# Half-row projections and query features, paired into two PSUM banks and issued as one burst per step

## The chip, the cores and the metric

The kernel runs on one core of a Trainium2 chip. The time is the device time of one execution in microseconds (us). The kernel before was timed beside every experiment of a call (one round of building and timing some kernels together), on the same chip; the calls ran on several chips, so a difference of two medians from different calls is rough. Its runs of one call spread by 2 to 5%, so verdicts rest on ratios: the mean time of one kernel's fast runs over the mean of the other's fast runs of the same rounds, with a 95% interval. That is not quite the ratio of the medians, which are quoted too. A run counts as slow when it lies over 1.5% above the fastest run of the same kernel; slow runs are in the medians, not in the ratios.

## The reference, cut to what matters

```python
def phi(x):                                    # x: q or k, (8 batches, 8 heads, 576 rows, 64)
    proj = np.einsum('bhsd,df->bhsf', x, w_phi)            # 64 -> 128
    proj = proj - np.max(np.abs(proj), axis=-1, keepdims=True)
    return np.concatenate([np.exp(proj), np.exp(-proj)], axis=-1)

q_p, k_p = phi(q), phi(k)
kv  = np.einsum('bhsf,bhsd->bhfd', k_p, v);  z = np.sum(k_p, axis=2)
num = np.einsum('bhsf,bhfd->bhsd', q_p, kv); den = np.einsum('bhsf,bhf->bhs', q_p, z)[..., None] + 1e-06
x = num / den                                  # then a second layer per batch, 512 wide:
h = np.maximum(x @ w_in, 0.0)                  # u and v are its halves
v_n = (v - mean) / np.sqrt(var + 1e-06)        # mean and var of v's rows
out = (u * (w_spatial @ v_n + b_spatial)) @ w_out
```

The contraction of each projection has 64 terms; TensorE has 128 rows.

## The kernel before

Work is cut into 36 units of eight 128-row blocks of q and k: 32 "pair" units (two heads of one batch, four blocks each) and 4 units of leftover rows (64 rows of each head, of two batches). Batches 0 to 7 have four units each; bN.j below is unit j of batch N, TN a unit of leftover rows. A step of the program handles one new unit, later parts of older units, and "fills" in matmuls of the second layer of finished batches. The turned q and k (kT, qT) hold two blocks one above the other, 64 rows each, and the weights are a block-diagonal matrix wphi2, so half of what TensorE multiplies is zero:

```python
def by_token(xT, half):                        # keys and queries alike
    ps = psum.tile([P, 4, F], FP32, tag="bank", name="ps")
    for x in range(2):
        nc.tensor.matmul(out=ps[:, 2 * x:2 * x + 2, :], lhsT=xT[:, 2 * half + x, :], rhs=wphi2, start=True, stop=True)
    return ps
...
def a_qfeat(u):                                # query features, and sel @ mT subtracts the row maxima
    for half in range(2):
        pq = psum.tile([P, 4, P], FP32, tag="bank", name="pq")
        for par in range(2):
            nc.tensor.matmul(out=pq[:, 2 * par:2 * par + 2, :], lhsT=wphi2[:, par * F:(par + 1) * F],
                             rhs=u["qT"][:, 2 * half:2 * half + 2, :], start=True, stop=False)
            ...                                # two matmuls with sel
        ...                                    # qf = exp(pq), exp(-pq) on ScalarE
...
ORDER = (("keys", 0.375), ("queries", 0.25), ("attention", 0), ("sums", 0.25),
         ("next", 0.125), ("features", 0), ("out", 0), ("maxima", 0))   # the number: share of the fill after it
```

After the keys come their row maxima on VectorE (mk), their exponentials on ScalarE (kf), and em = exp(-mk), exp(mk), with which GpSimd scales v (vs).

The inputs arrive in the background, by a table that counts in units ahead of their use. k and q are loaded by GpSimd's queue (which casts them to 2 bytes), v by SyncE's, and `cross` turns k and q of batches 2 to 7 by a DMA transpose on SyncE's queue into kT_b and qT_b:

```python
AT, AB, XP = 4, 5, 2
at(u["i"] - AT, load_tail, "k", u["g"]);   at(u["i"] - AT + 1, load_tail, "q", u["g"])   # leftover rows
at(u["i"] - AB, load, "k", u["b"]);        at(u["i"] - AB + 1, load, "q", u["b"])        # a batch
at(u["i"] - AB + 1, load_v, u["b"], nc.sync)
at(u["i"] - XP, cross, u["b"])
```

All PSUM tiles take turns in eight banks.

## Time and profile before

| | before |
|---|---|
| median of the first three runs | 289.92 us (286.92 to 296.59) |
| span in the profile | 286.4 us |
| PE / ScalarE / VectorE / GpSimd busy | 91% / 80% / 70% / 64% |
| last em (unit 35) starts at | 225.38 us |

PE's waits for loads (line, in total, times, longest), asked for from 60 us on to leave out the start, show one alone:

```profile
PE ps L232 <- DMA qT_b<-q_bf: 1.4, 1, 1.4
```

### The profile page before, as it was taken

The numbers are of one execution on the slowest core, as the hardware profiler recorded it, in microseconds if no ns is written. First come the engines' busy times: TensorE is split into PE (matmuls) and PEld (weight loads), VectorE is DVE, ScalarE is ACT, GpSimd is POOL, SyncE is SP. The second block draws the span as 40 slices with busy tenths as digits, with TensorE's granted clock in tenths as the row PEclk, the third lists the DMA queues.
The fourth block names the chain that finished last, engine by engine and source line by source line (L and its number), as shares of the span: only waits on it lengthen the run. The fifth ranks groups of instructions, "written<-read, shape, count | busy, mean of one in ns | idle before, by whom it ended". The sixth has DMA issues, their size and how long they took to land.

```text
span 286.4 us, 7965 instructions
## 1 busy us (share of the span) xinstructions
PE 261.6 (91%) x3070; PEld 178.6 (62%) x3070; DVE 201.8 (70%) x509; ACT 229.3 (80%) x517; POOL 182.2 (64%) x320
## 2 busy tenths in 40 slices
PE   1378889999999999999989999999999999999983
PEld 1157776777666776767557687666667676545441
DVE  4389997977958877598696887578688864354610
ACT  4949998899799988999998679799999746566033
POOL 8159998798336899479689954835969600058200
PEclk9999999999999999999999999999999999999999
DMA  6989999976568499999955994999111003500037
GB/s 185 203 171 120 206 219 223 163 203 71 79 147 186 102 187 155 173 245 196 130 94 102 225 191 87 264 287 255 32 22 32 7 2 122 211 3 0 0 90 242
DMA packets 81706, 40.31 MB, mean 141 GB/s; under 512 B 50242, under 2 KB 77058, under 8 KB 81668
## 3 DMA queue, kind: packets, MB, share of 16 engines
q1 hardware_dynamic: 54180, 28.32, 43.0%
q0 software_dynamic: 27328, 11.41, 35.5%
q8 instruction: 24, 0.39, 0.6%
q14 instruction: 14, 0.11, 0.2%
q10 hardware_dynamic: 160, 0.07, 0.1%
HBM read 32.85 MB, written 9.44 MB: 148 GB/s over the span
## 4 chain that ended last, share of the span: by engine, by line
PE 61%; ACT 14%; DVE 11%; DMA 9%; POOL 2%; issue 2%; ACTq 0%; SPq 0%; POOLq 0%; DVEq 0%
PE pv L403 10%; PE ps L477 8%; PE po L500 7%; PE pu L456 7%; PE ps L232 5%; ACT qf L321 5%; ACT kf L247 5%; PE pv L334 4%; DMA q_tl<-in_q_dram 4%; PE pn L354 4%; DMA out_dram<-ob 3%; PE pq L308 3%; PE pq L304 3%; DVE mk L244 3%; PE ps L478 2%; DVE mq L258 2%
## 5 line engine op out<-in xcount | busy, mean ns | idle before, releaser
L247 ACT ACTIVATE kf<-ps 128x512 bf16<-128x512 f32 x144 | 77.7, 692 | 5.6 <-DVE mk L244 5.4
L272 POOL TENSOR_TENSOR vs<-v_f,em 128x512 bf16<-128x512 f32 x64 | 65.6, 1049 | 23.6 <-ACT em L267 22.6
L321 ACT ACTIVATE qf<-pq 128x512 bf16<-128x512 f32 x128 | 68.2, 675 | 8.5 <-PE pq L308 8.5
L244 DVE TENSOR_REDUCE mk<-ps 128x4 f32<-128x512 f32 x72 | 46.1, 677 | 2.5 <-PE ps L232 2.0
L258 DVE TENSOR_REDUCE mq<-ps 128x4 f32<-128x512 f32 x62 | 39.9, 681 | 4.2 <-PE ps L232 3.4
L502 ACT COPY ob<-po 128x512 f32<-128x512 f32 (+1 forms) x37 | 21.6, 610 | 19.9 <-PE po L500 16.2
L406 DVE BATCH_NORM_STATS2 stats<-vr 128x6 f32<-128x512 bf16 (+1 forms) x37 | 24.8, 687 | 15.8 <-ACT vr L405 15.7
L477 PE MATMUL ps<-w_spT,vn 128*128 128x512 bf16 x128 | 32.8, 379 | 0.0
L456 PE MATMUL pu<-xT,w_in_bf 128*128 128x512 bf16 x128 | 31.6, 379 | 0.0
L403 PE MATMUL pv<-w_in_bf,xT 128*128 128x512 bf16 x128 | 31.2, 379 | 0.0
L480 DVE TENSOR_TENSOR uT<-ps,uT 128x512 bf16<-128x512 f32 x32 | 22.0, 689 | 12.7 <-PE ps L478 11.5
L500 PE MATMUL po<-w_out_bf,uT 128*128 128x512 bf16 x128 | 30.4, 379 | 0.0
L308 PE MATMUL pq<-mT,sel 128*128 128x128 bf16 x256 | 30.0, 219 | 0.0
L308 PEld LDWEIGHTS <-sel 128*128 128x128 bf16 x256 | 25.1, 98 | 3.9
L405 ACT ACTIVATE vr<-pv 128x512 bf16<-128x512 f32 (+1 forms) x37 | 23.3, 691 | 4.0 <-PE pv L403 3.9
L354 PEld LDWEIGHTS <-qf 128*128 128x128 bf16 x512 | 20.4, 97 | 8.2 <-issue 1.7
L345 DVE TENSOR_TENSOR x<-pn,rc 128x256 bf16<-128x256 f32 x64 | 25.0, 418 | 0.5
L420 POOL TENSOR_SCALAR vn<-vr,rs 128x512 bf16<-128x512 bf16 x32 | 24.3, 773 | 0.8
L334 PE MATMUL pv<-vs,kf 128*128 128x66 bf16 x512 | 24.5, 194 | 0.2 <-ACT kf L247 0.2
L354 PE MATMUL pn<-kv,qf 128*128 128x66 bf16 x512 | 22.3, 193 | 1.3 <-ACT qf L321 1.2
L334 PEld LDWEIGHTS <-kf 128*128 128x128 bf16 x512 | 21.7, 97 | 1.8 <-issue 0.9
L304 PE MATMUL pq<-qT_b,wphi 128*128 128x256 bf16 x96 | 22.4, 273 | 0.0
(120 smaller groups left out, 530.8 us busy)
## 6 DMA issues: line engine op xcount, KB each, us to landing
v_f<-in_v_dram SPq DMA_DIRECT2D x8, 1024.0 KB, 10.7
out_dram<-ob SPq DMA_DIRECT2D x32, 256.0 KB, 3.6
k_bf<-in_k_dram POOLq DMA_DIRECT2D x7, 512.0 KB, 7.0
q_bf<-in_q_dram POOLq DMA_DIRECT2D x7, 512.0 KB, 8.7
v_tl<-in_v_dram SPq DMA_DIRECT2D x8, 128.0 KB, 7.7
w_in_bf<-in_moe_w_in_dram POOLq DMA_DIRECT2D x2, 512.0 KB, 8.7
out_dram<-ob SPq DMA_DIRECT2D x8, 128.0 KB, 2.4
k_tl<-in_k_dram POOLq DMA_DIRECT2D x8, 64.0 KB, 6.8
```

The source lines that it names most:

```text
L244: nc.vector.tensor_reduce(out=u["mk"][:, hs], in_=pk, axis=AX.X, op=ALU.max, apply_absolute_value=True)
L247: nc.scalar.activation(out=u["kf"][:, s, hs, :], in_=pk, func=AF.Exp, bias=0.0, scale=sc)
L258: nc.vector.tensor_reduce(out=mq[:, 4 * half:4 * half + 4], in_=pq, axis=AX.X, op=ALU.max, apply_absolute_value=True)
L272: nc.gpsimd.tensor_tensor(out=vs[:, s, :, 0:D], in0=st[u["b"]]["v"][:, pj * H:(pj + 1) * H, :], in1=em[:, s, :].unsqueeze(2).to_broadcast( ...
L308: nc.tensor.matmul(out=pq[:, 2 * par + x, :], lhsT=sel[:, j, :], rhs=m, start=False, stop=(x == 1))
L321: nc.scalar.activation(out=qf[:, s], in_=pq, func=AF.Exp, bias=0.0, scale=sc)
L334: nc.tensor.matmul(out=pv[:, hh, s, :], lhsT=u["kf"][:, s, 4 * hh + c, :], rhs=u["vs"][:, s, 4 * hh + c, :], start=(c == 0), stop=False)
L354: nc.tensor.matmul(out=pn[:, pos, :], lhsT=u["qf"][hh][:, s, pos, :], rhs=d["kv"][:, 2 * u["pj"] + hh, s, :], start=(s == 0), stop=(s == 1))
L403: nc.tensor.matmul(out=pv[r], lhsT=lhs(kc), rhs=w_in_bf[:, kc, HALF:DFF], start=(kc == 0), stop=(kc == KC - 1))
L456: nc.tensor.matmul(out=pu, lhsT=w_in_bf[:, kc, dc * P:(dc + 1) * P], rhs=d["xT"][:, kc, :], start=(kc == 0), stop=(kc == KC - 1))
L477: nc.tensor.matmul(out=ps, lhsT=d["vn"][:, sp, cs], rhs=w_spT[:, sp, 0:T0], start=(sp == 0), stop=False)
L500: nc.tensor.matmul(out=po[r], lhsT=lhs(dc), rhs=w_out_bf[:, dc, :], start=(dc == 0), stop=(dc == KC - 1))
```

## The change

Its intent: contract over 64 rows only, two half-row matmuls side by side, each into a bank of its own; and, since a switch between full and half rows costs TensorE something, do all of a unit's half-row work at once at the head of a step (keys and queries of unit i, features of unit i-2), six banks in one burst. The reads of these banks are spread over the step. The core of the diff, with cuts marked:

```diff
+    def a_burst(uk, uf):
+        for u, x in ((uk, "k"), (uk, "q")):
+            u["p" + x] = [psum.tile([P, 4, F], FP32, tag="bank", name="ps") for par in range(2)]
+            for j in range(4):
+                for par in range(2):
+                    r = rows_of(par)                       # 64 rows
+                    nc.tensor.matmul(out=u["p" + x][par][:, j, :], lhsT=u[x + "T"][r, j, :],
+                                     rhs=wphi2[r, par * F:(par + 1) * F], start=True, stop=True)
+        ...                                                # features: two of 512 columns, then sel, 4 pairs
-    ORDER = (("keys", 0.375), ("queries", 0.25), ("attention", 0), ("sums", 0.25),
-             ("next", 0.125), ("features", 0), ("out", 0), ("maxima", 0))
+    ORDER = (("burst", 0), ("keys0", 0.125), ("queries", 0.125), ("feat0", 0.25), ("maxima", 0.125),
+             ("attention", 0), ("next", 0), ("keys1", 0), ("sums", 0.125), ("feat1", 0), ("out", 0.25))
-    EARLY = 5                                              # units whose maxima VectorE splits, not GpSimd
+    EARLY = 7
-    load_v(0, nc.sync)                                     # ahead of the leftover rows
...                                                        # leftover rows, and k and q, heads 2 and 3
+    load_v(0, nc.gpsimd)
...                                                        # vst1 and vnt1 are cleared at step 8, not at the start
-    AT, AB, XP = 4, 5, 2
+    AT, AB, XP = 4, 6, 3                                   # first group (batches 2, 3): still 5 and 2; v: still 4
```

## The prediction

> **What bounds the kernel now.** I read the page's busy shares first, then the busy time of the engines stage by stage, then ScalarE's timeline, then the chain of PE work. A unit is eight 128-row blocks of q and k; there are 36 (32 "pair" units, 4 of leftover rows), and a step of the program handles one new unit and fills in matmuls of the second layer.
>
> ```profile
> PE 261.6 (91%) x3070; PEld 178.6 (62%) x3070; DVE 201.8 (70%) x509; ACT 229.3 (80%) x517; POOL 182.2 (64%) x320
> ```
>
> By this line PE is the bound and ScalarE has 20% to spare. The stages say something else:
>
> ```profile
> 122.00:152.00 30.00, 28.10 (x352) 19.48 (x350) 24.38 (x64) 29.32 (x70) 24.95 (x47) 1.00 1.00 158
> 152.00:175.00 23.00, 23.00 (x303) 16.79 (x301) 19.59 (x42) 17.92 (x43) 15.87 (x28) 1.00 1.29 184
> 226.00:286.40 60.40, 55.18 (x485) 30.38 (x481) 25.06 (x61) 28.26 (x51) 14.61 (x27) 1.00 0.24 79
> ```
>
> Columns: stretch, its length, then PE, weight loads, DVE, ACT, POOL. From 122 to 152 us ScalarE is busy 29.3 of 30 us: there it sets the pace. From 152 to 175 us PE is busy all 23 us and ScalarE 17.9: there PE does. After 226 us there are almost no projections left, only the second layer on PE. ScalarE's timeline shows both kinds of step:
>
> ```profile
> 131.24 2.25 ACT L458 ACTIVATE uT<-pu 128x512 bf16<-128x512 f32 x4
> 133.35 2.09 ACT L321 ACTIVATE qf_t<-pq 128x512 bf16<-128x512 f32 x4
> 135.26 2.14 ACT L247 ACTIVATE kf<-ps 128x512 bf16<-128x512 f32 x4
> 137.18 0.41 ACT L267 ACTIVATE em<-mk 128x8 f32<-128x8 f32 x2
> ...
> 156.64 0.38 ACT L267 ACTIVATE em<-mk 128x8 f32<-128x8 f32 x2
> 157.43 0.38 ACT L339 CAST kv<-pv 128x264 bf16<-128x264 f32 x1 [0.41 <-PE pv L336]
> 158.94 1.57 ACT L321 ACTIVATE qf<-pq 128x512 bf16<-128x512 f32 x3 [1.14 <-PE pq L308]
> ```
>
> In the first four lines each group starts where the one before hands over (133.35 to 135.26 is 1.91 us for four exponentials, 0.48 each): no idle. In the last lines it idles 0.41 and 1.14 us for PE. The chain of work gives PE's real rates (a start-to-start time, unlike the mean of one instruction, which contains its latency):
>
> ```profile
> 152.29 0.11 PE pq L304
> 152.40 0.11 PE pq L308 x2
> ...
> 153.23 0.44 PE ps L232 x4
> 153.66 0.86 PE ps L477 x4
> 154.53 0.21 PE ps L478
> 154.74 0.44 PE ps L232 x4
> 155.18 0.86 PE ps L477 x4
> 156.04 0.22 PE ps L478
> 156.26 0.50 PE pn L354 x16
> ```
>
> The features (L304 and L308, four such pairs of rows) take 4 x 0.22 = 0.88 us, the key and query projections 0.44 each: 1.76 us per unit is what the change touches. All of it multiplies a zero half: wphi2 is block-diagonal, 64 useful rows of 128.
>
> **What the Trainium skill says.** "TensorEngine Tiling (Array Packing)", Overview and Tiling Modes: a contraction of 64 rows can run as two 64-row tiles at once, up to 2x, and changing the mode drains TensorE. "TensorE: Matmul & The Clock Gate", Part 3: matmuls of different row groups run concurrently, and a weight load overlaps a running matmul if its row group differs. No run of before has such pairs, so its trace can't confirm either; it does show that a 128-column weight load hides at the rate of 0.50 us / 16 = 31 ns per load and matmul. "TensorEngine Tiling", Gotcha 1: row tiles must write different PSUM banks, and tiling does not speed up evacuation. The change obeys the first half, and the second half is my main argument. "PSUM — Partial Sum Buffer", Terms: two engines may not read one bank at a time; the trace agrees in that exponentials of keys wait for VectorE's reduction of the same bank (kf after mk, 5.4 us over 4 waits, shown below).
>
> **The change part by part.**
>
> 1. *Half rows.* Keys become 8 matmuls of 128 columns in 4 pairs instead of 4 of 256, queries likewise, the features two of 512 side by side, the maxima (sel) 8 of 128 in 4 pairs. The built program has 3270 matmuls instead of 3070 and the same 577,920 output columns: if pairs did not overlap, nothing would be saved. If they do, a pair costs 128 columns = half of 0.11 us = 0.055, but needs two weight loads at 31 ns, so 0.062: keys 0.25, queries 0.25, sel 0.25; the wide pair takes 512 columns, 0.22. Together 0.97 instead of 1.76, so 0.79 less. I give back 0.1 (an estimate of mine) for two mode changes per step, which is also why all is in one burst. Net 0.7 us per unit, 25 us of PE work over 36 units.
>
> 2. *What of it is on the path.* In ScalarE-bound steps nothing: its work per step stays (8 exponentials x 0.48, two em 0.2, kv 0.26, three or four fill tasks x 0.48, near 6 us). What can go is ScalarE's idle time in which it waited for PE. From 12 to 226 us that was, after the view of waits, qf 6.1, kv 2.1, qf_t 1.8, ob 0.8, kT 0.8, vr 0.7, uT 0.5, uTt 0.3 = 13.1 us. A PE-bound step goes from 6.16 us (152.29 to 158.47 between features) to about 5.4, still above ScalarE's 4.4, so not all idle goes; I take 70%, 9 us.
>
> ```profile
> ACT qf L321 <- PE pq L308: 6.1, 7, 1.2
> ACT kf L247 <- DVE mk L244: 5.4, 4, 3.3
> ACT kv L339 <- PE pv L336: 2.1, 5, 0.7
> ```
>
> 3. *The end.* After the last numerator matmul both programs have the same 92,224 columns on PE: untouched. Before it, three feature groups stand on PE at 227, 232 and 238 us, each 0.4 us shorter: 1.2 us.
>
> 4. *The start.* ScalarE clears vst1 and writes vnt1 before the first exponential; this moves to step 8 (the memset to VectorE):
>
> ```profile
> 8.69 1.95 ACT L61 COPY vst<-zero 128x2112 bf16<-128x2112 bf16 x1
> 10.54 1.13 ACT L61 COPY vnt<-ident 128x512 bf16<-128x512 bf16 x2
> 11.58 2.05 ACT L247 ACTIVATE kf<-ps 128x512 bf16<-128x512 f32 x4
> ```
>
> So the first exponential can start 2.9 us sooner. The 1 MB load of v moves behind the tail rows and the next k and q, for which PE waited (k_tl 3.4, q_tl 1.8 us). Against it: vnt1's 1.1 us comes back on ScalarE later, and VectorE is busy 19.2 of the 20 us from 20 to 40 and gets more early work (EARLY 7 for 5). Net 3 us.
>
> 5. *Loads of k and q for later batches* one step earlier: PE's one wait of 1.4 us for qT_b may go. 1 us.
>
> 6. *Given back:* six of eight banks are taken at the head of a step. By the build's bank numbers, in a ScalarE-bound step the burst's last bank is freed by the previous step's last qf, but one or two finished fill tiles stand before ScalarE then, so it should not run dry. I give back 2 us.
>
> Sum: -9 - 1.2 - 3 - 1 + 2 = -12.2, on a span of 286.4: 274.2, a ratio of 0.957. Of the median 289.92 that is 277.5. The three runs of before spread by 3%, so the ratio counts more than the figure.
>
> **The rivals.**
>
> *Pairs do not overlap* (each load waits for the running matmul, or the switch drains long). Then PE still does 577,920 columns plus 200 more instructions; only the start is gained: near 286, "same". For it: nothing in before shows concurrency. Against it: the skill's statement, and two banks per pair chosen for it.
>
> *The burst starves ScalarE.* Keys' second half is read late, pf banks later still; if PE stands at the head of each step for a bank, ScalarE runs dry perhaps 0.3 us in each of 33 steps, 10 us, and the gain is gone: 285 to 288. For it: before, about two banks were asked for at a time. Against it: my walk through the bank numbers above, and ScalarE has work from 6 banks after a burst.
>
> *PE was the bound everywhere, as the page's 91% suggests.* Then 25 us go at once: about 262 of 286.4, or 265. Against it: ScalarE's timeline without gaps from 122 to 150 and 187 to 226 us, and its 229 us of work, plus an end that does not shrink.
>
> *VectorE or the loads set the start anyway:* then part 4 gives 0 to 1 us, 279.5.
>
> **Range and chances.** 277.5 us. The first two rivals, and the fourth, reach up; the third and a larger gain at the start reach down. 271 to 285 should hold it 8 times in 10. Faster by over 2% (under 284.1) 0.79, within 2% 0.18, slower 0.03.
>
> **What would show it.** Key and query projections at about 0.25 us per eight matmuls, the burst near 1.0 us; PE-bound stretches at about 5.4 us per step; ScalarE over 95% in the stretches where it was so before, with step lengths unchanged; first key exponential near 8.7 us; the end from the last numerator on as long as before, within 0.5 us. Wrong if the pairs start one after the other's end, if ScalarE shows waits for pk or pf at each step's head, or if ScalarE-bound steps get shorter too.

## More of the kernel before

The prediction shows the lines for PE and ScalarE. What it does not show are two rows of the page that cut the span in 40 slices of 7.2 us: the clock granted to TensorE and the busy share of the 16 DMA engines, both in tenths.

```profile
PEclk9999999999999999999999999999999999999999
DMA  6989999976568499999955994999111003500037
```

The clock is full throughout. The DMA engines are at least 90% busy from 7 to 14 us, from 21 to 57, from 100 to 143, from 158 to 172 and from 179 to 200 us.

## The result, and the profile after

The changed kernel gives the right result in 302.65 us (median, 301.25 to 306.76, 4 runs); the kernel before beside it took 290.71 us (286.92 to 296.59). The ratio of the fast runs is 1.0478, interval [1.0327, 1.0628]: slower. The profiled run is a fast one, with a span of 299.5 us. Its page:

```profile
PE 255.5 (85%) x3270; PEld 156.1 (52%) x3270; DVE 203.6 (68%) x517; ACT 228.1 (76%) x514; POOL 182.9 (61%) x317
...
PEclk9999999999998999799999995999999999999999
DMA  9959999941969699999802999889911101600026
```

PE is busy for 6 us less, as half rows should make it, and every engine has a smaller share of a longer span: the time went into waiting. Three slices of the clock's row are low, and each lies at a wait of PE for a load. The waits from 60 us on, to set beside the single line of before:

```profile
PE pt L227 <- DMA q_tl<-in_q_dram: 7.5, 2, 5.1
PE ps L244 <- DMA kT_b<-k_bf: 2.4, 1, 2.4
PE ps L244 <- DMA qT_b<-q_bf: 1.2, 1, 1.2
```

These three come to 11.1 us instead of 1.4 (0.6 us in two other waits for transfers are left out). Where the time was lost is read from the starts of em in the two traces (the last column is after less before, and its sum is the difference of the spans):

| stretch | before, us | after, us | difference |
|---|---|---|---|
| start to em of unit 1 | 19.0 | 18.6 | -0.4 |
| units 2 to 4 | 12.7 | 14.8 | +2.1 |
| units 5 to 8 | 20.9 | 23.0 | +2.1 |
| units 9 to 13 (T1, b2.0 to b2.3) | 34.8 | 33.7 | -1.1 |
| units 14 to 17 (b3.0 to b3.3) | 24.0 | 28.5 | +4.5 |
| units 18, 19 (T2, b4.0) | 13.8 | 18.3 | +4.5 |
| units 20 to 26 (b4.1 to b5.3) | 43.7 | 41.2 | -2.5 |
| unit 27 (T3) | 6.7 | 13.4 | +6.7 |
| units 28 to 35 | 49.7 | 48.7 | -1.0 |
| last em to the end | 61.0 | 59.3 | -1.7 |

The first and last rows need care, because em stands near the head of a step before and near its end after. The key projections stand at the head of a step in both. By their starts the change is 2.4 us ahead at unit 1 (13.34 against 15.70 us), 0.6 behind at unit 9 (57.05 against 56.41), and from those of unit 35 to the end it takes 64.1 us instead of 64.6. So the start loses less than the table says; most of the loss lies between.

The half rows themselves do what they were meant to do. PE's timeline (start, time that the group spans):

```profile
167.36 0.38 PE L480 MATMUL ps<-w_spT,vnt 128*128 128x512 bf16 x1
167.67 0.40 PE L244 MATMUL ps<-wphi,kT_b 64*128 64x128 bf16 x8
167.90 0.39 PE L244 MATMUL ps<-wphi,qT_b 64*128 64x128 bf16 x8
...
168.34 0.39 PE L256 MATMUL pf<-mT,sel 64*128 64x128 bf16 x8
168.66 1.04 PE L479 MATMUL ps<-w_spT,vn 128*128 128x512 bf16 x4
...
173.19 0.40 PE L244 MATMUL ps<-wphi,kT_b 64*128 64x128 bf16 x8
```

Eight half-row matmuls, four pairs, take 0.23 us from start to start (167.67 to 167.90), where four full ones took 0.44; the burst takes 0.99 us up to the next fill (168.66); the step takes 5.52 us (167.67 to 173.19), where the prediction's PE-bound step of before took 6.16. The third group of leftover rows, some steps on, shows where the time went instead:

```profile
176.91 0.39 PE L227 MATMUL pt<-ident,k_tl 128*128 128x128 bf16 x4
182.35 0.59 PE L227 MATMUL pt<-ident,q_tl 128*128 128x128 bf16 x4 [5.06 <-DMA q_tl<-in_q_dram]
...
186.10 0.61 PE L244 MATMUL ps<-wphi,kT 64*128 64x128 bf16 x8
186.50 0.64 PE L244 MATMUL ps<-wphi,qT 64*128 64x128 bf16 x8
```

PE stands still for 5.06 us until q_tl has landed, and afterwards it is slow: the same eight matmuls take 0.40 us (186.10 to 186.50). The windows of the stall and of the 7 us after it (columns as in the prediction; the last three are clock, DMA share, GB/s):

```profile
177.00:183.00 6.00, 0.94 (x16) 0.79 (x13) 1.67 (x8) 2.37 (x7) 3.08 (x4) 0.81 1.55 159
183.00:190.00 7.00, 7.00 (x109) 5.58 (x107) 3.61 (x7) 2.78 (x7) 0.41 (x2) 0.68 1.24 153
```

The clock in the second is 0.68 of full, with PE busy throughout. As an estimate, 7 us at 0.68 lose 7 x 0.32 = 2.2 us, so this stall cost almost half as much again as it lasted. "TensorE: Matmul & The Clock Gate", Part 1, describes just this in the Trainium skill: a wait for a DMA long enough to count as idle brings the clock down, and the next matmuls start slow. The trace agrees.

Why did q_tl come late? The chain of work through this place, in order of time:

```profile
167.68 0.90 POOL q_bf L61
...
171.91 10.31 DMA q_tl<-in_q_dram
```

GpSimd issued the load of q for batch 6 (512 KB) at 167.68 us and the leftover rows q_tl, two loads of 64 KB, 3.5 us later; at 171.18 us SyncE issued the turning of k of batch 6. q_tl took 10.31 us among them; before, such a load took 6.2 us in the median, 4.0 to 11.4 in all. The Trainium skill, "DMA: Bandwidth & Descriptors", says under "Issuing engines are not separate DMA queues" that DMAs issued by different engines run on the same 16 DMA engines and interleave. The trace agrees in that this small load, from GpSimd's queue, was slow while SyncE's turning ran; whether the turning or the load of q ahead of it held it up, the trace doesn't separate. In the kernel before, the load of q for batch 6 comes just after q_tl instead of before it, and nothing waits.

At the start the first exponential of the keys comes when predicted, and its gain is gone two units later (ScalarE, then GpSimd):

```profile
8.68 2.07 ACT L270 ACTIVATE kf<-ps 128x512 bf16<-128x512 f32 x4 [0.22 <-DVE mk L266]
...
14.71 1.08 ACT L270 ACTIVATE kf<-ps 128x512 bf16<-128x512 f32 x2 [3.77 <-DVE mk L266]
```
```profile
17.78 2.04 POOL L294 TENSOR_TENSOR vs<-v_f,em 128x512 bf16<-128x512 f32 x2 [6.57 <-DMA v_f<-in_v_dram]
```

ScalarE started 2.9 us sooner and then waited 3.77 us for the leftover rows; GpSimd waited 6.57 us for v, which had been moved back.

### The profile page after: what moved, and what is told of

It is laid out like the page before. It is cut to its first block, busy times and chain, and to the rows that moved or that the text cites.

```text
span 299.5 us, 8370 instructions
## 1 busy us (share of the span) xinstructions
PE 255.5 (85%) x3270; PEld 156.1 (52%) x3270; DVE 203.6 (68%) x517; ACT 228.1 (76%) x514; POOL 182.9 (61%) x317
## 4 chain that ended last, share of the span: by engine, by line
PE 31%; ACT 21%; DMA 17%; POOL 12%; DVE 11%; issue 6%; SPq 0%; ACTq 0%; POOLq 0%; DVEq 0%
ACT kf L270 7%; DMA q_tl<-in_q_dram 7%; ACT qf L323 6%; PE pv L405 5%; PE po L502 5%; PE ps L479 5%; PE pu L458 4%; ACT vr L407 3%; POOL vs L294 3%; POOL vn L422 3%; DVE mk L266 3%; DMA q_bf<-in_q_dram 3%; DMA xT<-x 3%; DMA qT_b<-q_bf 2%; DMA out_dram<-ob 2%
## 5 line engine op out<-in xcount | busy, mean ns | idle before, releaser
L270 ACT ACTIVATE kf<-ps 128x512 bf16<-128x512 f32 x144 | 84.2, 648 | 20.9 <-DVE mk L266 18.9
L323 ACT ACTIVATE qf<-pf 128x512 bf16<-128x512 f32 x144 | 84.5, 657 | 4.6 <-PE pf L256 4.5
L266 DVE TENSOR_REDUCE mk<-ps 128x4 f32<-128x512 f32 x72 | 48.8, 680 | 16.6 <-PE ps L244 14.3
L504 ACT COPY ob<-po 128x512 f32<-128x512 f32 (+1 forms) x37 | 22.8, 625 | 21.3 <-PE po L502 18.1
L278 DVE TENSOR_REDUCE mq<-ps 128x4 f32<-128x512 f32 x58 | 37.5, 675 | 0.0
L405 PE MATMUL pv<-w_in_bf,xT 128*128 128x512 bf16 x128 | 32.6, 395 | 0.4 <-DMA xT<-x 0.2
L336 PEld LDWEIGHTS <-kf 128*128 128x128 bf16 x512 | 22.6, 100 | 2.2 <-issue 1.1
L338 PE MATMUL pv<-vst,kf 128*128 128x66 bf16 x128 | 21.8, 195 | 1.0 <-POOL vst L311 1.0
L460 ACT ACTIVATE uT<-pu 128x512 bf16<-128x512 f32 x32 | 20.9, 653 | 2.2 <-PE pu L458 2.0
L309 POOL TENSOR_TENSOR vst<-v_tl,em 64x512 bf16<-64x512 f32 x16 | 16.3, 1038 | 7.7 <-ACT em L289 7.4
```

The lines of the kernel that those rows point to most:

```text
L266: nc.vector.tensor_reduce(out=u["mk"].rearrange("p (j two) -> p j two", two=2)[:, :, par], in_=pk, axis=AX.X, op=ALU.max, apply_absolute_v ...
L270: nc.scalar.activation(out=out, in_=pk, func=AF.Exp, bias=0.0, scale=sc)
L278: nc.vector.tensor_reduce(out=mq.rearrange("p (par j) -> p par j", par=2)[:, par], in_=u["pq"][par], axis=AX.X, op=ALU.max, apply_absolute ...
L323: nc.scalar.activation(out=qf[:, s], in_=u["pf"][par], func=AF.Exp, bias=0.0, scale=sc)
L336: nc.tensor.matmul(out=pv[:, hh, s, :], lhsT=u["kf"][:, s, 4 * hh + c, :], rhs=u["vs"][:, s, 4 * hh + c, :], start=(c == 0), stop=False)
L405: nc.tensor.matmul(out=pv[r], lhsT=lhs(kc), rhs=w_in_bf[:, kc, HALF:DFF], start=(kc == 0), stop=(kc == KC - 1))
```

## The experiments

The first reading of the two traces gave this theory: the change lost its time to loads that come too late for it. Rivals: the half rows or the burst cost time by themselves (switches, banks held), or the start does. The letters in an expectation belong to its own call. Where a kernel is said to be wrong, it reads old data; its time is meant, not its result. For the first call no ratios were computed: the kernel before took 293.17 us (286.73 to 296.75, 7 runs), and only one of its runs counts as fast, so the first four experiments are read from medians and traces. In the other calls its median was 290.62 to 291.20 us.

### Loads: the table changed

**a_loads_as_before**: the changed kernel with the old table.

```diff
-    AT, AB, XP = 4, 6, 3
+    AT, AB, XP = 4, 5, 2
```

> The changed kernel with the timing of the later batches' k and q loads and of their DMA transposes as before (each one step later than the change has them), nothing else. Theory D (the loss is PE standing 2.9 and 5.1 us for q_tl at the third and fourth group of leftover rows, and running at a lower clock after it, because the transposes now run beside that load): about 292, and the two steps that took 11.1 and 13.4 us fall to 7 to 8 us. Theory B (the burst takes six banks and starves ScalarE in every step): unchanged, 300 to 303.

297.13 us (295.31 to 301.17; the profiled run was a slow one). The waits for q_tl are gone, and T2 and T3 take 6.82 us each instead of 11.07 and 13.39. But PE now waits 5.5 us in four places for qT_b and 5.0 in three for kT_b: b4.0 takes 10.15 us and b7.0 11.47. About 5.5 us of the loss belong to the table, and the old table is not a cure.

**a_cross_later** and **a_tail_earlier**: one entry of the table each.

```diff
-    AT, AB, XP = 4, 6, 3
+    AT, AB, XP = 4, 6, 2        # a_cross_later: k and q turned one unit later
+    AT, AB, XP = 6, 6, 3        # a_tail_earlier: leftover rows two units earlier
```

> The changed kernel with only the DMA transposes of later batches one step later, as before; loads of k and q stay one step early. Theory D with the transposes as the rival of q_tl: about 292 to 294. If instead the early k and q loads delay q_tl: near 300. Theory B: 300 to 303.

303.36 us (300.45 to 305.17): as the changed kernel. PE waits 6.7 us for kT_b, 4.2 for qT_b and 3.5 for q_tl.

> The changed kernel with the loads of the leftover rows of the third and fourth group two steps earlier, transposes as changed. Theory D: no wait of PE for q_tl any more, about 290 to 293, lower than with the transposes later. Theory B: 300 to 303.

298.59 us (297.65 to 300.26). No wait for q_tl is left, but one of 4.6 us for kT_b at b3.0, and b5.2 takes 11.72 us. With each entry another load becomes the late one.

**b_loads_as_after**: the kernel before with the table of the change.

```diff
-    AT, AB, XP = 4, 5, 2
+    AT, AB, XP = 4, 6, 3        # first group still 5 and 2, v still 4, as in the change
```

> The kernel before with the load and transpose timing of the change (one step earlier for later batches). Theory D in its strong form (the timing alone costs): 295 to 300 and PE waits for q_tl. Theory B, or D only together with the change's later issue on POOL: within 2% of before, 287 to 292.

291.70 us (290.55 to 295.59), with the kernel before at 293.17: no effect shows in the medians, and with a single fast run of the kernel before (286.73) a fair ratio can't be formed. Its trace has three short waits of PE for transfers, of 0.9, 0.8 and 0.6 us, at full clock. So the table alone doesn't bring the loss in the old order of a step, while it costs some 5.5 us in the new one; something in the new step makes the kernel sensitive to it.

### Loads: the later ones taken away

**a_no_later_loads** and **b_no_later_loads**, wrong: units of batches 4 to 7, and leftover rows of groups 2 and 3, read what earlier batches loaded.

```diff
+        if u["g"] > 1 and not u["pair"]:
+            gs[u["g"]] = dict((x, gs[1][x]) for x in ("q", "k", "v"))
+        if u["pair"] and u["b"] > 3 and u["pj"] == 0:
+            st[u["b"]] = dict((x, st[u["b"] - 2][x]) for x in ("kT", "qT", "v"))
...
-        if u["pair"] and u["pj"] == 0 and u["g"] > 0:      # and the same for the leftover rows
+        if u["pair"] and u["pj"] == 0 and u["g"] == 1:
```

> The changed kernel with no loads and no DMA transposes of k, q, v for batches 4 to 7 and the last two groups of leftover rows: they use the tiles of batches 2 and 3 and of group 1 again (the result is wrong on purpose; all arithmetic stays). Theory D (late loads): PE's DMA waits of the second half go, and with them about 11 us: near 290, with the third and fourth group's steps at about 7 us. Theory B (the burst starves ScalarE): 299 to 303.

289.81 us (287.91 to 290.57, 20 runs), ratio 0.9972 [0.9947, 0.9996]: 12.8 us under the changed kernel. PE still waits 3.5 us for kT_b and qT_b of batch 3, whose loads were not taken away.

> The kernel before with the same loads taken away (result wrong on purpose). It waits little for loads, so both theories say at most 3 us less than before: 286 to 291. What tells is its ratio to the changed kernel without those loads: near 1 (or the changed one faster after the start) under theory D, 4 to 5% apart under theory B.

285.86 us (284.43 to 286.40), ratio 0.9832 [0.9780, 0.9884]: 4.9 us under the kernel before. So these loads cost the change 8 us more than they cost the kernel before. The starts of em agree: without later loads, T2 and T3 take 6.83 and 6.82 us in the changed kernel.

These two runs also tell how much the half rows are worth when nothing arrives late. Units 18 to 35 in both (before, then changed; the lengths of the windows are the times from em of unit 18 to em of unit 35):

```profile
118.30:221.70 103.40, 101.99 (x1262) 72.90 (x1276) 82.54 (x203) 98.68 (x236) 72.08 (x134) 1.00 0.20 52
```
```profile
127.00:229.30 102.30, 96.81 (x1360) 59.98 (x1375) 81.96 (x202) 98.16 (x234) 73.01 (x135) 1.00 0.20 51
```

PE's busy time falls by 5.2 us, the stretch by 1.1. ScalarE is busy for 98.68 of 103.4 and 98.16 of 102.3 us, 95 and 96%: it sets the pace, and there were at most 4.7 us of its idle time to win in half of the kernel.

### The parts of the change: rows, burst, start

**a_spread**: half rows of the change, with its start and its table, but at the old places of a step, in the old order. **a_full_rows**: the burst of the change on full rows, without pairs.

```diff
 # a_spread
-    ORDER = (("burst", 0), ("keys0", 0.125), ("queries", 0.125), ("feat0", 0.25), ...
+    ORDER = (("keys", 0.375), ("queries", 0.25), ("attention", 0), ("sums", 0.25),
+             ("next", 0.125), ("features", 0), ("out", 0), ("maxima", 0))
 # a_full_rows
-                    r = rows_of(par)
+                    r = slice(0, P)
```

> The changed kernel with its half-row matmuls in the places where the matmuls stood before: keys, queries and features apart, each with its own two banks, and the order and fill shares of before; loads and start as changed. Theory B: the burst was the fault, so 288 to 293. Theory D: the loads stay late, 297 to 304, perhaps 2 to 4 us worse by two more mode changes per step.

297.28 us (293.72 to 299.17), ratio 1.0155 [1.0069, 1.0241], against 1.0478 for the change (two fast runs here): in this setting the burst is worth some three points of the loss, even though nothing of its own work is longer. Start and table together cost 1.6 points here, over the half rows alone (b_half_rows below, 0.9997), though the table had shown no effect in the old order.

> The changed kernel with all its projections, features and maxima on full 128 rows (the other half of the weights' rows is zero; the maxima are subtracted twice, which cancels in the quotient), one after the other instead of two side by side. If pairs overlap as the rates in the trace suggest (keys 0.23 us for eight), the burst grows from about 1.1 to 1.9 us; if PE were what sets the time this costs 20 to 25 us (325), if it only does so in the PE-bound steps 8 to 12 us (311), and if overlap is worth nothing, 302.

305.90 us (303.22 to 308.10), ratio 1.0446 [1.0374, 1.0518]; the profiled run was slow. The changed kernel's 1.0478 lies inside this interval: in this order of a step, half rows or full rows make no difference that these runs could show.

**a_start_mended**: the changed kernel with v's first load and EARLY as before. **a_no_loads_start_mended**: the same without later loads, wrong.

```diff
+    load_v(0, nc.sync)           # ahead of the leftover rows
-    load_v(0, nc.gpsimd)
-    EARLY = 7
+    EARLY = 5
```

> The changed kernel with the first load of v back at its place of before (ahead of the leftover rows, on the other queue) and the early units counted to 5 as before; the rest of the change stays. Theory S (the start costs some 6 us of the 13 lost: v comes late, and VectorE, back to back there, is given more): the exponentials of em of unit 5 go from 37.9 to about 36 us or less, of unit 8 from 56.4 to about 52.5, and the time falls by about 5 us to 297. Rival (the DMA engines are full in the first 45 us, so whatever is put first pushes something else back): unit 8 stays at 55 to 57 us, the time at 300 to 303.

301.66 us (299.83 to 303.60), ratio 1.0397 [1.0345, 1.0449]. The theory of the start falls: em of unit 8 starts at 57.6 us, where it foretold 52.5. GpSimd still waits 4.7 us for v, and PE 4.7 us for the leftover rows k_tl. The rival, that what is put first pushes something else back, is what happened.

> Both suspected costs taken away at once: the changed kernel without the later batches' loads (wrong result on purpose) and with the start mended as in the run before. If start and loads are the whole loss, what is left of the change is its gain: 289.8 less 5 to 6 is about 284, at or below the kernel before without its later loads (285.9). If the burst itself costs time (theory B), it stays at 287 to 290.

289.90 us (288.19 to 290.75), ratio 0.9987 [0.9943, 1.0030], the same as without the mending (289.81). This is what theory B, a burst that costs by itself, foretold; the 284 us of the other theory, that start and later loads are the whole loss, did not come. But the loads of batch 3 are still in, with waits of 2.0 and 1.2 us; the last two experiments take them away too.

**b_start_deferred**: the kernel before with vst1 and vnt1 cleared at step 8, and one load of the weights instead of two.

```diff
-    for i in range(2):
-        nc.scalar.dma_start(out=wphi_f[i * D:(i + 1) * D, :], in_=w_phi)
+    nc.scalar.dma_start(out=wphi_f, in_=bass.AP(tensor=w_phi.tensor, offset=w_phi.offset, ap=[[0, 2], [F, D], [1, F]]))
...
+    at(8, pin(nc.vector.memset), vst[1], 0.0)     # instead of the start
+    at(8, ones_rows, 1)
```

> The kernel before with one part of the change: the clearing of the second pair of tiles put off to step 8 and one load of the projection's weights instead of two. Everything else, v's load too, stays. If the start's gain is real and was lost to v's place and the early units: first exponential of the keys near 8.7 us, and the time 1.5 to 3 us below the kernel before, 288 to 289. If loads or VectorE set the start in any case (the fourth rival of the prediction): within 0.7 us of the kernel before.

292.64 us (290.70 to 295.13), ratio 1.0082 [1.0025, 1.0138]: 0.8% slower, which neither theory foretold (its profiled run was slow; the start is read from it all the same). The first exponential comes at 8.35 us, as in the change, and the second set gains nothing:

```profile
16.89 2.06 ACT L246 ACTIVATE kf<-ps 128x512 bf16<-128x512 f32 x4 [6.29 <-DVE mk L243]
```

ScalarE waits 6.29 us for the maxima of the leftover rows, for which k_tl has to land; em of unit 1 starts at 18.81 us instead of 19.02. Here the transfer sets the start, not ScalarE. And the clearing comes back at T1 and b2.0, which take 17.28 us together instead of 15.64.

**a_all_earlier**: the start mended, and every later load asked for earlier.

```diff
-    AT, AB, XP = 4, 6, 3
+    AT, AB, XP = 6, 8, 3         # first group 5 and 6 instead of 4 and 5
```

> The start mended and every later load asked for earlier: leftover rows 6 units ahead instead of 4, k and q 8 instead of 6, the turned copies 3. If the loads only came too late: PE's waits for q_tl, kT_b and qT_b go, and the time is 288 to 291, as before the change. If the DMA engines are too full for the new rhythm, one load moved earlier pushes another back: 294 to 299, with at least one PE wait of 3 us or more for a load.

306.20 us (304.59 to 307.20), ratio 1.0550 [1.0504, 1.0595], worse than either theory expected. Two waits are left, but long ones, both at batch 3: 6.2 us for kT_b and 4.1 for qT_b; b3.0 takes 15.38 us. Its turning was issued at 92.2 and 95.9 us, among the loads of batch 4 that were moved up (k at 85.0, q at 93.0 us). Asking sooner is no cure where the transfers are already dense.

### Half rows alone, the burst alone

These four have start, EARLY and table of the kernel before; only the order of the step differs, and all have half rows.

**b_half_rows**: the old places (ORDER as in a_spread). **a_burst_alone**: the burst. **a_burst_keys_first**: the burst, with both halves of the keys read, and em computed, right after it. **a_burst_queries_late**: the burst without the query projections, which stand after the first half of the keys.

```diff
 # a_burst_keys_first
-    ("keys0", 0.125), ("queries", 0.125), ... ("next", 0), ("keys1", 0), ("sums", 0.125)
+    ("keys0", 0), ("keys1", 0.125), ("queries", 0.125), ... ("next", 0), ("sums", 0.125)
 # a_burst_queries_late (shortened)
-        for u, x in ((uk, "k"), (uk, "q")):
+        for u, x in ((uk, "k"),):
...
             elif what == "queries" and uk:
+                a_burst(uk, None, "q")
```

> The kernel before with the half rows alone: pairs into two banks, but at the old places of a step, with the old order, the old start and the old timing of loads. If the half rows are sound and worth little (ScalarE sets the pace of most steps): ratio 0.985 to 1.00, about 1 to 3 us under the kernel before. If the half rows themselves cost time (two banks at once, more instructions, switches three times a step): ratio above 1.005.

288.86 us (287.48 to 294.80, 22 runs), ratio 0.9997 [0.9961, 1.0032]. The half rows alone show no cost and no gain among fast runs. A small gain isn't excluded: the medians differ by 2.3 us (288.86 and 291.20), since 14 of 27 runs of the kernel before count as slow, and 2 of 22 of these.

> Half rows and the burst, with start, early units and timing of loads of the kernel before: only the order within a step differs from the run above. If the burst's order makes the loads late (theory B): ratio 1.015 to 1.03, with PE waits of 3 us or more for kT_b or qT_b. If start and load table of the change were the cause: ratio under 1.005.

297.27 us (295.89 to 299.73), ratio 1.0267 [1.0181, 1.0352]. The burst alone costs 8.4 us over the half rows at their old places. Waits of PE from 60 us on, half rows at the old places first, then the burst:

```profile
PE ps L243 <- DMA qT_b<-q_bf: 2.4, 2, 2.1
PE ps L243 <- DMA kT_b<-k_bf: 0.3, 1, 0.3
```
```profile
PE ps L245 <- DMA kT_b<-k_bf: 4.3, 3, 2.0
PE ps L245 <- DMA qT_b<-q_bf: 3.0, 3, 1.4
```

The mean clock is 0.977 in the second and 1.000 in the first. No single wait reached the 3 us that I had expected; it is six of them, and what they bring after them. By the starts of the key projections the burst is 0.7 us ahead at unit 9 (57.16 against 57.89), and behind by 4.1 at unit 18 and by 6.6 at unit 35.

ScalarE's waits show one more thing that the burst changes (half rows at the old places, then the burst, whole runs):

```profile
ACT qf L322 <- PE pf L255: 11.9, 10, 1.7
ACT kf L269 <- DVE mk L265: 7.5, 5, 5.3
```
```profile
ACT kf L271 <- DVE mk L267: 18.9, 18, 3.4
ACT qf L324 <- PE pf L257: 6.5, 6, 1.5
```

It waits 5.4 us less for the features on PE, and 11.4 us more for VectorE's row maxima of the keys. From 60 us to the last em (60 to 227 us) the old places have no such wait for maxima, the burst has 10.1 us, and 8.9 us even without loads (a_burst_no_loads below).

> As the run above, but both halves of the keys are read, and em computed, right after the burst instead of at the end of the step. If the loads come late because em, and so GpSimd's products vs and the loads that GpSimd issues after them, stand half a step later (theory G): k_bf of the last batch is issued about 3 us earlier in its step, PE's waits for kT_b and qT_b shrink, and the time falls by 4 us or more under the run above. If it is the need at the head of the step (theory H): no change, within 2 us.

305.83 us (302.30 to 307.41), ratio 1.0519 [1.0418, 1.0619]. This theory falls: instead of gaining 4 us the kernel loses 8.6, with a wait of 6.1 us for qT_b. An earlier em doesn't make up for the loss, so its late place isn't shown to be what makes the loads late.

> As the second run of this call, but the query projections are taken out of the burst and come at their own place, after the keys. Theory H (the burst needs kT_b and qT_b both at the head of a step, where the kernel before needed the queries some 2 us later): PE's waits for qT_b shrink and the time falls by 3 us or more under the second run. Theory G: within 2 us of it.

293.10 us (292.37 to 296.29), ratio 1.0134 [1.0044, 1.0225]: 4.2 us less, half of the burst's cost, as the theory of the need at the head of the step asked; the two intervals overlap somewhat. Its own mark failed, though: PE's waits for qT_b stay at 2.9 us (3.0 before), and those for kT_b fall from 4.3 to 2.3. So taking queries out of the burst helps; that it helps by a later need of qT_b is not shown.

**b_half_rows_no_loads** and **a_burst_no_loads**, wrong: the first two of these four without any load from batch 3 on.

```diff
+        if u["pair"] and u["b"] > 2 and u["pj"] == 0:
+            st[u["b"]] = dict((x, st[2][x]) for x in ("kT", "qT", "v"))
...
-        if u["pair"] and u["pj"] == 0 and u["g"] > 0:
+        if u["pair"] and u["b"] == 2 and u["pj"] == 0:
```

> Half rows at the old places, with start and load table of the kernel before, but no loads from the fourth batch on (they read earlier data again: wrong result on purpose). 282 to 286 us, 3 to 6 under the half rows with loads (288.9), as the kernel before gained 4.9 us from the same cut one batch later.

284.63 us (283.34 to 285.81), ratio 0.9805 [0.9764, 0.9847].

> Half rows in a burst, start and load table of the kernel before, and the same cut. Theory L (the burst costs only through its loads, which it needs sooner than they come): its 8.4 us over the half rows at the old places (297.3 to 288.9) shrink to 0 to 3 us, most of them at the start, so 283 to 288 us. Rival (the burst costs by itself: banks held, maxima late, GpSimd late): 6 to 8 us stay, 289 to 293 us.

286.50 us (285.85 to 287.29), ratio 0.9875 [0.9837, 0.9914]. The difference between burst and old places is 1.9 us without these loads and 8.4 with them, and from 60 us on PE waits for no load in either. By the starts of the key projections, the burst is 1.2 us ahead at unit 9 (58.17 against 59.42 us) and 0.6 behind at unit 35 (220.26 against 219.65); em, which stands later in the step of the burst, would hide this (57.50 against 55.75 us at unit 8). The spans of the two profiled runs differ by 0.6 us only. The rival, that the burst costs by itself through banks, late maxima or a late GpSimd, foretold 289 to 293 us and falls. One limit: the cut takes away more than late landings. GpSimd no longer issues these loads, and SyncE no longer turns k and q, so what the burst loses to those isn't told apart.

No kernel that was tried beats the kernel before by more than the noise: the best right one is b_half_rows.

## Why the prediction was wrong

The prediction said 277.5 us with a range of 271 to 285; the kernel took 302.7. By its own steps:

1. *Half rows* were right. 0.23 us per eight matmuls for 0.25, a burst of 0.99 us for 0.97, a PE-bound step of 5.52 us for 5.4. The first rival, pairs that don't overlap, is out.
2. *What of it is on the path*: wrong in size. The step "I take 70%, 9 us" should have read 0 to 2: half rows alone have a ratio of 0.9997, and medians 2.3 us apart. Seven tenths of the 13.1 us of ScalarE's waits for PE were counted as gain, as if less work on PE would shorten them; with half rows at the old places ScalarE still waits 7.2 us for the features between 60 and 227 us, for 7.0 before. In the burst these waits do shrink, but waits for VectorE's maxima take their place. With nothing arriving late, the second half of the kernel is ScalarE's for 95 to 96% of the time and gains 1.1 us. That ScalarE-bound steps would keep their length was right (units 20 to 23: 23.9 us for 23.8).
3. *The end* was right where it was claimed exactly: from the start of the last numerators it takes 45.2 us (254.30 to 299.5) for 44.9 (241.48 to 286.4). The 1.2 us before it didn't come: from the key projections of unit 35 the rest is 0.4 us shorter (64.1 for 64.6). From the last em it is 1.7 us shorter, but em stands at another place of the step.
4. *The start*: wrong. The first exponential at 8.68 us came as foretold; the step "Net 3 us" failed. By the key projections 2.4 us are gained at unit 1 and 0.6 lost at unit 9. The deferral alone, in the kernel before, made it 0.8% slower, and the burst with the old start reaches unit 9 at the same time (57.16 for 57.05). The fourth rival, that VectorE or the loads set the start anyway, was the right one.
5. *Loads one step earlier*: wrong in sign, and the prediction had not thought that a table could cost anything. "1 us" to gain became 5.5 us lost (302.65 to 297.13 with the old table).
6. *Given back*: wrong in size and in kind. "I give back 2 us" for PSUM banks became 8.4 us for the burst, of which 6.5 go away with the loads. The second rival described a ScalarE starved by PE's waits for banks at the head of each step; without late loads the burst costs 1.9 us, so that isn't the loss. It was near in one point: the sign "ScalarE shows waits for pk or pf at each step's head" came in another form, as waits for VectorE's maxima of pk (8.9 us without loads).

In sum, in medians: 288.9 us with half rows alone, +8.4 for the burst, +5.4 for the load table (297.27 to 302.65), about 0 for start and EARLY together (a_burst_alone, with the old start, takes what a_loads_as_before takes with the new one, 297.27 and 297.13). That accounts for the changed kernel along this path; the parts don't simply add, for in the old order start and table cost more (8.4 us from b_half_rows to a_spread, 288.86 to 297.28) than these figures say. The prediction also took the skill's remark that tiling doesn't speed up evacuation for its "main argument" and was right in it; the page has it under "PSUM Bottleneck", not under Gotcha 1.

Shown: most of the burst's loss, 6.5 of 8.4 us, goes away with the loads, and half rows lose nothing and gain at most about 2 us. Argued only: how the burst makes the loads late. It needs kT and qT at once at the head of a step, and PE's stalls then lower its clock; but of two experiments on how it does so, one failed and one moved the time without moving the wait that it was about. Which of the order's shifts delays which transfer stays open, and so does where the last 1.9 us lie.

What I should have seen before: the page's row of DMA at 90% or more for two fifths of the time, and a wait of 1.4 us for one transfer. Both stood in the profile of the kernel before, and the prediction counted them as a possible gain.

## What to carry to other kernels

Before an order of work is changed, write down for each background transfer when it lands and when it is first needed; where that margin is near zero and the DMA engines are full, a change that frees an engine can still lose, and a load that is moved up pushes another back. Test the parts of a change one by one, and run the same pair of kernels once without their loads: the difference that goes away belongs to the loads and to issuing them. When two orders of a step are compared, mark time by something that stands at the same place in both. A bound engine's idle time is a limit for a gain, not an estimate of it: another wait can take its place.

## What the Trainium skill lacked or had wrong

- "TensorEngine Tiling (Array Packing)", Key Properties, says that a change of tiling mode drains TensorE, without a figure. Here a full-row matmul of 512 columns has 0.31 us to the first half-row one (167.36 to 167.67), where the next full one follows after 0.21 (169.54 to 169.75), and the last eight of the burst take 0.32 us to the next full one, where eight others take 0.23: about 0.1 us each way in this step.
- The same page's speedup of up to 2x for 64 rows held: 0.23 us for 0.44, with the two halves of a pair in banks of their own. That the whole kernel gained next to nothing from it is what "PSUM Bottleneck" on that page leads one to expect, as ScalarE reads these banks and was 95% busy.
- "TensorE: Matmul & The Clock Gate", Part 1, fits: after a wait of 5.06 us the granted clock was 0.68 over the next 7 us. It can also fall after a shorter wait, and late: PE waited 0.42 and then 2.45 us for leftover rows, until 121.8 us; the first matmuls after that still ran at the usual pace (five in 0.16 us, 122.00 to 122.16), and the clock was 0.67 from 122 to 124 us and 0.50 from 124 to 126.
- "DMA: Bandwidth & Descriptors" has no figure for a small transfer beside large ones: two loads of 64 KB took 10.31 us here from issue to landing, beside the load of a batch and a DMA transpose, where the median in the kernel before is 6.2 us (4.0 to 11.4).
